# Twice the margin of zero matmuls against the TensorE clock gate, paced by ScalarE, also into the emptied P.V bank

## Chip, cores, metric

The kernel runs on one core of a Trainium2 chip. The metric is the device time of one execution in microseconds (us), as a median over timed executions. The granted clock of TensorE is 1.000 at full speed. PE is TensorE, ACT is ScalarE, DVE is VectorE, POOL is GpSimd. All kernels in this document gave correct outputs.

## The reference, cut to what matters

There are two identical layers on a sequence of 2048 rows of 512: multi-query attention with 32 heads of 16, then a gated MLP that mixes over the sequence.

```python
x = x + _A_ref(_layernorm(x), wq, wk, wv, wo)       # 32 heads, one K and one V of width 16
x = x + _B_ref(_layernorm(x), w_in, w_sp, b_sp, w_out)
x = x + _A_ref(_layernorm(x), wq, wk, wv, wo)
x = x + _B_ref(_layernorm(x), w_in, w_sp, b_sp, w_out)
# _A_ref: scores = q k^T / 4, p = softmax(scores), o = p v, then o @ wo
# _B_ref: z = gelu(x @ w_in); z1, z2 = halves; g = w_sp @ layernorm(z2) + b_sp; (z1 * g) @ w_out
```

The exponentials (32 x 2048 x 2048 in each layer) are the bulk of the work.

## The kernel before

The program is not written by hand in order. A list scheduler in the kernel file holds a model of five engines, with an assumed duration for every operation. It simulates them and emits each engine's instructions in the order in which the model started them. PE's list gets its scores (`fill`), the products P.V (`pv`), the background matmuls (projections and the mix over the sequence), and a filler: multiplications of a zero matrix, whose only purpose is to keep PE busy enough for full clock.

```python
TICK = 3.4133            # us, the window in which the model counts PE's columns
TICK_COLS = 3060.0       # columns in a window that the model takes to be enough for full clock
...
def below(self, t, lim):
    # earliest time from t on at which the columns of the last TICK us are under lim
    ...
    return t
...
WARM = 800.0             # margin over TICK_COLS
...
class WarmStream:        # the zero matmuls
    def peek(self, f):
        ...
        t = sc.below(f, TICK_COLS + WARM)
        if u >= len(k.units) or k.units[u].first:       # between two groups: P.V is being emptied
            free = [b for b in sc.banks if not b.busy and not b.closed and b.free_at <= t]
            if not free:
                return None                             # no bank to write to: no zeros
            self.bank = free[0]
        if not sc.fast(t):
            return (t, -1.0)                            # priority: ahead of everything
        return (t, 0.6)                                 # ahead of most background matmuls

    def commit(self, t):
        ...             # inside a group a zero matmul adds zero to P.V's own bank
        pace = []
        if t > k.sc.free["pe"] + 0.3:
            pace = [d for en in ("act", "dve") for d in k.sc.order[en][-8:] if t - 1.5 < d.vis <= t]
            pace = sorted(pace, key=lambda d: -d.vis)[:1]
        o = k.sc.op("pe", fn, 512 / 2400.0, [k.c_zero] + pace + ..., 9.0, sem="warm")
```

`pace` makes a zero matmul wait for the operation that the model finished last before it, so that zeros don't run off early. ACT exponentiates three or two score blocks of 128x512 at a time out of two rings in PSUM. DVE takes about one block in eight and computes it by a polynomial, for which it reads the scores (line L1558) and runs five more instructions for each pair of blocks.

The softmax here doesn't subtract the row's maximum and nothing guards it: scores larger than these inputs give would overflow.

Of the kernel before, what the change touches and what calls it, by code (L numbers as in the profile page):

```python
# [28 lines left out]
TICK_COLS = 3060.0  # L29
# [28 lines left out]
class Sched:  # L58
# [96 lines left out]
        return o  # L155

    def _arm(self, o):
        o.ready = max([d.end if d.eng == "pe" and o.eng == "pe" else d.vis for d in o.deps], default=0.0)
        self.ready[o.eng].append(o)
        self.cache.pop(o.eng, None)  # L160
        for e, _f, _d in o.alts:
            self.ready[e].append(o)
            self.cache.pop(e, None)
# [4 lines left out]
    def _pick(self, eng):  # L168
# [3 lines left out]
        for o in self.ready[eng]:  # L172
# [8 lines left out]
            if r < INF:  # L181
                late = o.unit is not None and o.unit < self.unit_now() + NEAR
                cands.append((r, 0.1 if late else o.prio, o.seq, o, 0.0))
# [187 lines left out]
NDB = 2  # L371

LOOK = 8
NEAR = 4
URGENT = 1.0
BACKLOG = 3.0
WARM = 800.0
ENDX = 6
PR_LAST = 0.3
PR_SMALL = 0.6  # L380
# [6 lines left out]
def d_psum(n):  # L387
    return n * 1.042e-3 + 0.066
# [6 lines left out]
def d_act(n):  # L395
    return n * 0.8333e-3 + 0.051
# [27 lines left out]
class Kern:  # L424
    def __init__(self, nc, A_x, A_wq, A_wk, A_wv, A_wo, B_x, B_w_in, B_w_sp, B_b_sp, B_w_out, out):
# [15 lines left out]
        sc = self.sc = Sched([5, 7])  # L441
# [67 lines left out]
        self.evac_n = 0  # L509
        self.hT_read = [[], []]  # L510
        self.pv_evac = None

        self.load(A_x, A_wq, A_wk, A_wv, A_wo, B_b_sp)
        self.fill_s = FillStream(self)
# [29 lines left out]
        return self.ps16[:, 1024 * b:1024 * (b + 1)]  # L544

    def transpose(self, out, src, deps, sem, pr):
        return self.sc.op("sp", lambda e: e.dma_start_transpose(out, src), 1.2, deps, pr, sem=sem, dma=131072, lat=0.9)

    def dma(self, fn, deps, sem, nbytes, prio=5.0, eng="sp", issue=0.5):
        return self.sc.op(eng, fn, issue, deps, prio, sem=sem, dma=nbytes)  # L550
# [77 lines left out]
    def ln(self, tiles, deps_t, dst, dst_deps, pr, urgent=False, on_pe=False):  # L628
        sc = self.sc
        n = len(tiles)  # L630
        t0 = tiles[0]
        ag = []
        for t in tiles:
            s_ = sc.op("dve", lambda e, t=t: e.bn_stats(self.st1[:, t, :], self.X[:, t, :]), 0.6, deps_t(t),  # L634
                       pr + 0.5)
            ag.append(sc.op("dve", lambda e, t=t: e.bn_aggr(self.mv1[:, t, :], self.st1[:, t:t + 1, :]), 0.13, [s_],
                            pr + 0.4))
        a = sc.op("dve" if urgent else "pool", lambda e: e.tensor_scalar(
            self.ve1[:, t0:t0 + n], self.mv1[:, t0:t0 + n, 1], LN_EPS, None, op0=ALU.add), 0.08 if urgent else 0.25, ag, pr)
        r = sc.op("pool", lambda e: e.tensor_tensor(self.rs1[:, t0:t0 + n], self.ve1[:, t0:t0 + n],  # L640
                                                    self.mhalf[:, 0:1].to_broadcast([P, n]), ALU.pow),
                  0.3 + 0.17 * n, [a, self.c_mh], pr)
        xo = []
        slots = []
        for t in tiles:
            sl = self.xn_n % 4
            self.xn_n += 1
            slots.append(sl)
            xo.append(sc.op("dve", lambda e, t=t, sl=sl: e.tensor_scalar(
                self.xn[:, sl, :], self.X[:, t, :], self.mv1[:, t, 0:1], self.rs1[:, t:t + 1], op0=ALU.subtract,  # L650
                op1=ALU.mult), 0.22, [r, self.last_xn[sl]], pr + 0.3))

        if not urgent and not on_pe:
            evs = []
            for i, (t, sl) in enumerate(zip(tiles, slots)):
                o = self.transpose(dst[:, i, :, :], self.xn[:, sl, :], [xo[i]] + dst_deps, f"xt{sl}", pr)
                self.last_xn[sl] = o
                evs.append(o)
            return evs

        def pe(e, b):
            ins = None
            for i, sl in enumerate(slots):
                for kd in range(KD):
                    k = i * KD + kd
                    ins = e.transpose(self.b16(b)[:, k * 128:(k + 1) * 128], self.xn[:, sl, kd * 128:(kd + 1) * 128],
                                      self.ident[:])
            return ins

        def cp(b):  # L670
            return dst, self.b16(b)[:, 0:n * 512].rearrange("p (t kd c) -> p t kd c", t=n, kd=KD)
        pt, (ev,) = sc.job([(pe, n * 4 * 0.06)], [dict(
            fn=lambda e, b: e.tensor_copy(*cp(b)), dur=d_psum(n * 256), prio=pr, deps=dst_deps,
            alts=[("act", lambda e, b: e.activation(*cp(b), ACTF.Copy), d_act(n * 512) + 0.1)])], xo + [self.c_id], pr)
        for sl in slots:
            self.last_xn[sl] = pt
        return [ev]
# [240 lines left out]
    def mixer_chunk(self, g):  # L918
        sc = self.sc
        n = g.n  # L920
        nt = n // 128
        T = [g.t0 // 128 + i for i in range(nt)]
        last = (g.ci == len(self.chunks) - 1)
        pr = PR_LAST if last else (PR_SMALL if g.ci >= 3 else 3.0)
# [9 lines left out]
        for i, t in enumerate(T):  # L934
            for h in range(2):
# [8 lines left out]
                def cp(b, t=t, h=h):  # L944
# [6 lines left out]
                                         deps=list(self.z2_read.get(t, ())),  # L951
# [16 lines left out]
        for f0 in range(0, NF, per):  # L968
# [10 lines left out]
            def cp(b, f0=f0, m=len(fs)):  # L979
# [5 lines left out]
                                for i in range(0, len(mm), w)],  # L985
                               [con] if last else [dict(fn=lambda e, b, cp=cp: e.tensor_copy(*cp(b)), dur=d_psum(n * len(fs)), prio=pr - 1,  # L986
                                     deps=z1_war,
# [12 lines left out]
        nt = len(T)  # L1000
# [16 lines left out]
        for ci, (zt, zn, v) in zip(batch, zs):  # L1017
            sp = self.dma(lambda e, zt=zt, zn=zn, v=v: e.dma_start(self.z1_dv[:, :, zt * 128:zt * 128 + zn], v), z1,
                          f"z1s{g.layer}{zt}", zn * P * NF * 2)
# [9 lines left out]
        for t in T:  # L1029
# [3 lines left out]
        a = sc.op("dve" if last else "pool", lambda e: e.tensor_scalar(  # L1033
            self.ve2[:, T[0]:T[0] + nt], self.mv2[:, T[0]:T[0] + nt, 1], LN_EPS, None, op0=ALU.add), 0.08 if last else 0.25,
            ag, pr)
        r = sc.op("pool", lambda e: e.tensor_tensor(self.rs2[:, T[0]:T[0] + nt], self.ve2[:, T[0]:T[0] + nt],
                                                    self.mhalf[:, 0:1].to_broadcast([P, nt]), ALU.pow),
                  0.3 + 0.17 * nt, [a], pr)
        for t in T:
            self.z2_op[t] = sc.op("dve", lambda e, t=t: e.tensor_scalar(  # L1040
                self.z2n[:, t, :], self.z2n[:, t, :], self.mv2[:, t, 0:1], self.rs2[:, t:t + 1], op0=ALU.subtract,
# [201 lines left out]
class FillStream:  # L1243
# [26 lines left out]
    def peek(self, f):  # L1270
        k = self.k
        r = self.n % 2
        if self.pending[r]:
            return None
        self.blocks = self.nxt(k.ring[r][1])
        if not self.blocks:
            return None
        deps = [self.exp_of[r]]
        for b in self.blocks:
            g = b.unit.grp  # L1280
            if g.q.op is None or g.q.op.start is None:
                return None
            deps.append(g.q.op)
            o = k.k_op.get((g.layer, b.unit.kt))
            if o is None or o.start is None:
                return None
            deps.append(o)
        if not k.sc.reclaim(r):
            return None
        self.deps = [d for d in deps + k.sc.lent_rel(r) if d is not None]  # L1290
        return (max([d.vis for d in self.deps], default=0.0), 0.0)
# [173 lines left out]
class DexStream:  # L1465
# [28 lines left out]
    def take(self, t, js):  # L1494
# [27 lines left out]
        layer = k.units[fu].grp.layer  # L1522
        u = max(self.u, fu + LOOK)
        while u < len(k.units):
# [117 lines left out]
class WarmStream:  # L1642
# [10 lines left out]
    def peek(self, f):  # L1653
        k = self.k
        sc = k.sc
        u = k.pv_s.u
        self.bank = None
        if sc.nleft == 0 or k.c_zero.start is None:
            return None
        f = max(f, k.c_zero.vis)  # L1660
        t = sc.below(f, TICK_COLS + WARM)
        if u >= len(k.units) or k.units[u].first:
            free = [b for b in sc.banks if not b.busy and not b.closed and b.free_at <= t]
            if not free:
                return None
            self.bank = free[0]
        if not sc.fast(t):
            return (t, -1.0)
        return (t, 0.6)

    def commit(self, t):
        k = self.k
        b = self.bank

        def fn(e):
            return e.matmul(k.b32(k.pvb if b is None else b.idx), k.zero[:], k.zero[:, None, :].to_broadcast([P, 4, P]),  # L1676
                            start=b is not None, stop=b is not None)
        pace = []
        if t > k.sc.free["pe"] + 0.3:
            pace = [d for en in ("act", "dve") for d in k.sc.order[en][-8:] if t - 1.5 < d.vis <= t]  # L1680
            pace = sorted(pace, key=lambda d: -d.vis)[:1]
        o = k.sc.op("pe", fn, 512 / 2400.0, [k.c_zero] + pace + (b.rel if b is not None else []), 9.0, sem="warm")
        k.sc.commit(o, t)
        if b is not None:
            b.rel = [o]
            b.free_at = o.end
        self.n += 1
# [59 lines left out]
```

## Time and profile before

| | before |
|---|---|
| timed executions when the prediction was made | 1846.22 us median of 3 (1843.32 to 1848.53) |
| the profiled execution | 1860.4 us (span 1858.4 us, granted clock 0.983) |
| zero matmuls | 786 |
| ACT busy in the profiled execution | 1746.0 us of 1858.4 |

These lines are from the page of the profiled execution of before: busy time by engine, the granted clock in 40 slices (tenths), and two of the costliest groups (busy us, mean ns | idle time ahead of them, and what ended it).

```profile
span 1858.4 us, 30069 instructions
...
PE 1599.4 (86%) x11874; PEld 473.0 (25%) x11874; DVE 1700.6 (92%) x2912; ACT 1746.0 (94%) x1570; POOL 52.4 (3%) x90
...
PEclk9899999999999999998999999999999999999999
...
L1374 ACT ACTIVATE Pa<-ps_all 128x1536 bf16<-128x1536 f32 (+1 forms) x1433 | 1631.8, 1372 | 32.6 <-PE ps_all L1694 30.8
...
L1676 PE MATMUL ps_all<-zero 128*128 128x512 bf16 x786 | 257.8, 399 | 34.9 <-DVE mv L1032 7.2
...
```

ACT is 94% busy. Its exponentials (L1374) take 1631.8 us and wait 30.8 us for scores. The clock row is 8 in two slices only; its tenths hide most of what is below 1.

The next lines are busy times in seven stretches of the same execution: first:last us and length, then PE, weight loads, DVE, ACT and POOL, each busy (xinstructions), then PEclk, the DMA share and GB/s. The stretches are the start, the first 16 groups of attention, groups 17 to 24 (here the first gelus and layer norms of the mixer come in between), the rest of the first layer, the first 8 groups of the second layer, the rest of its attention, and the last stage.

```profile
...
0.00:14.40 14.40, 11.39 (x70) 5.12 (x70) 13.02 (x37) 6.88 (x14) 7.29 (x20) 1.00 0.92 286
14.40:426.90 412.50, 335.93 (x2654) 91.28 (x2653) 391.56 (x632) 406.47 (x364) 5.75 (x11) 0.98 0.19 49
426.90:656.00 229.10, 204.78 (x1457) 57.32 (x1457) 205.33 (x338) 220.12 (x186) 6.62 (x6) 0.96 0.08 23
656.00:922.80 266.80, 240.80 (x1741) 80.44 (x1740) 230.92 (x433) 239.71 (x226) 10.17 (x18) 0.98 0.17 46
922.80:1154.20 231.40, 188.10 (x1424) 52.51 (x1422) 210.65 (x361) 214.62 (x201) 5.94 (x12) 0.99 0.06 14
1154.20:1805.90 651.70, 571.40 (x4271) 164.09 (x4272) 605.58 (x1011) 641.41 (x552) 15.49 (x22) 0.99 0.10 28
1805.90:1858.40 52.50, 47.02 (x262) 22.27 (x260) 43.59 (x109) 16.84 (x34) 1.10 (x2) 1.00 0.32 97
...
```

The same view in windows of 3.41 us shows one cold spell:

```profile
...
51.20:54.61 3.41, 2.85 (x29) 0.76 (x27) 3.31 (x5) 3.13 (x4) 0.00 (x0) 1.00 1.15 346
54.61:58.02 3.41, 2.08 (x15) 0.35 (x12) 3.34 (x6) 2.70 (x3) 0.00 (x0) 0.70 1.11 280
58.02:61.43 3.41, 3.41 (x15) 0.62 (x11) 3.27 (x5) 2.37 (x3) 0.00 (x0) 0.50 1.15 306
61.43:64.85 3.42, 3.42 (x21) 0.64 (x18) 1.08 (x2) 2.77 (x3) 0.00 (x0) 0.50 1.15 307
64.85:68.26 3.41, 3.21 (x31) 0.67 (x27) 3.11 (x5) 3.15 (x3) 0.00 (x0) 0.80 1.14 304
...
```

The half clock comes on within the second row and goes off within the last one. ACT has 0.7, 1.0, 0.6 and 0.3 us idle in these four windows. Over the whole execution 30 such windows are below full clock; ACT is idle 20.0 us in them. The spells are at half clock and last 3.41, 6.83 or 10.24 us; the cuts above don't lie on their borders, so more cuts are touched.

Two causes of such spells are seen in the timeline (start us, length us, engine, line, operation; in brackets the idle time before it and what ended it). Here zeros wait for a late DVE:

```profile
...
515.11 0.39 PE L1676 MATMUL ps_all<-zero 128*128 128x512 bf16 x1
515.55 3.47 DVE L1040 TENSOR_SCALAR z2n<-z2n,mv,rs 128x896 bf16<-128x896 bf16 x8 [1.56 <-POOL rs L1036]
...
517.38 0.61 PE L1676 MATMUL ps_all<-zero 128*128 128x512 bf16 x1 [1.89 <-DVE z2n L1040]
...
517.92 0.61 PE L1694 MATMUL ps_all<-qs,kT 32*128 32x512 bf16 x3
...
518.58 1.45 ACT L1374 ACTIVATE Pa<-ps_all 128x1536 bf16<-128x1536 f32 x1 [1.59 <-PE ps_all L1694]
...
```

The zero at 517.38 waits 1.9 us for DVE's normalization. The scores (L1694) stand behind it on PE although ACT had read out their bank by 516.1 us, and ACT idles 1.59 us. The Trainium skill ("TensorE: Matmul & The Clock Gate", Part 2, step 1) says that matmuls stay in program order and only weight loads are pulled ahead; this trace agrees.

The other cause is a boundary between two groups, here PE alone. P.V's bank is being emptied, no zero is placed between the scores, and PE idles 0.95 and 0.52 us of two; the clock falls behind it:

```profile
...
148.95 0.39 PE L1694 MATMUL ps_all<-qs,kT 32*128 32x512 bf16 x3
150.29 0.39 PE L1694 MATMUL ps_all<-qs,kT 32*128 32x512 bf16 x4 [0.95 <-ACT Pa L1374]
151.21 0.39 PE L1694 MATMUL ps_all<-qs,kT 32*128 32x512 bf16 x2 [0.52 <-ACT Pa L1374]
...
152.50 1.03 PE L1676 MATMUL ps_all<-zero 128*128 128x512 bf16 x2
...
```

### The profile page before, as it was taken

The numbers are of one execution on the slowest core, as the hardware profiler recorded it, in microseconds if no ns is written. First come the engines' busy times: TensorE is split into PE (matmuls) and PEld (weight loads), VectorE is DVE, ScalarE is ACT, GpSimd is POOL, SyncE is SP. The second block draws the span as 40 slices with busy tenths as digits, with TensorE's granted clock in tenths as the row PEclk, the third lists the DMA queues.
The fourth block names the chain that finished last, engine by engine and source line by source line (L and its number), as shares of the span: only waits on it lengthen the run. The fifth ranks groups of instructions, "written<-read, shape, count | busy, mean of one in ns | idle before, by whom it ended". The sixth has DMA issues, their size and how long they took to land.

```text
span 1858.4 us, 30069 instructions
## 1 busy us (share of the span) xinstructions
PE 1599.4 (86%) x11874; PEld 473.0 (25%) x11874; DVE 1700.6 (92%) x2912; ACT 1746.0 (94%) x1570; POOL 52.4 (3%) x90
## 2 busy tenths in 40 slices
PE   8878788778899999998887787987887899899998
PEld 3221222122222222222431211221122222222324
DVE  8999999999988999985869999999999998998868
ACT  8999999999999999999569999999999999999983
POOL 2000000000000000000010000000000000000000
PEclk9899999999999999998999999999999999999999
DMA  9700010001000021101120000100010000112013
GB/s 271 200 1 1 9 38 1 1 1 23 17 24 24 24 46 44 47 35 55 48 51 1 1 1 5 42 1 1 1 21 15 29 24 26 44 43 72 10 55 110
DMA packets 122963, 68.02 MB, mean 37 GB/s; under 512 B 76996, under 2 KB 119240, under 8 KB 122824
## 3 DMA queue, kind: packets, MB, share of 16 engines
q1 hardware_dynamic: 121240, 65.95, 13.2%
q8 instruction: 94, 1.54, 0.3%
q14 instruction: 45, 0.37, 0.1%
q10 hardware_dynamic: 1584, 0.16, 0.1%
HBM read 30.97 MB, written 17.83 MB: 26 GB/s over the span
## 4 chain that ended last, share of the span: by engine, by line
ACT 39%; DVE 21%; PE 20%; issue 17%; DMA 1%; POOL 1%; ACTq 0%; SPq 0%; POOLq 0%
ACT Pa L1374 38%; PE ps_all L1694 5%; PE ps_all L1116 5%; DVE E L1558 3%; PE ps_all L1450 3%; DVE Pd L1589 3%; DVE E L1587 2%; DVE E L1583 2%; DVE E L1585 1%; PE ps_all L1676 1%; PE ps_all L1208 1%; DVE st L634 1%; PE ps_all L939 1%; DVE gp L1129 1%; DVE st L1030 1%
## 5 line engine op out<-in xcount | busy, mean ns | idle before, releaser
L1374 ACT ACTIVATE Pa<-ps_all 128x1536 bf16<-128x1536 f32 (+1 forms) x1433 | 1631.8, 1372 | 32.6 <-PE ps_all L1694 30.8
L1694 PE MATMUL ps_all<-qs,kT 32*128 32x512 bf16 x4096 | 567.9, 389 | 186.9 <-ACT Pa L1374 173.2
L1558 DVE TENSOR_SCALAR E<-ps_all 128x512 f32<-128x512 f32 x514 | 351.1, 685 | 32.3 <-PE ps_all L1694 28.9
L1694 PEld LDWEIGHTS ps_all<-qs,kT 32*128 32x128 bf16 x4096 | 139.0, 91 | 751.7 <-ACT Pa L1374 691.2
L1450 PE MATMUL ps_all<-Pa,V 128*32 128x512 bf16 x3582 | 326.3, 391 | 0.0
L1589 DVE SCALAR_TENSOR_TENSOR Pd<-E 128x1024 uint16<-128x1024 f32 x259 | 313.5, 1211 | 4.2
L1676 PE MATMUL ps_all<-zero 128*128 128x512 bf16 x786 | 257.8, 399 | 34.9 <-DVE mv L1032 7.2
L1116 PE MATMUL ps_all<-wsT,z2n 128*128 128x512 bf16 x714 | 200.3, 383 | 1.5 <-DVE E L1558 0.5
L1450 PE MATMUL ps_all<-Pd,V 128*32 128x512 bf16 x514 | 182.4, 391 | 0.0
L1585 DVE TENSOR_TENSOR E<-E 128x1024 f16<-128x1024 f16 x259 | 176.6, 682 | 4.7
L1587 DVE TENSOR_TENSOR E<-E 128x1024 f16<-128x1024 f16 x259 | 176.6, 682 | 4.2
L1583 DVE TENSOR_SCALAR E<-E 128x1024 f16<-128x1024 uint16 x259 | 176.6, 682 | 1.6
L1586 DVE TENSOR_SCALAR E<-E 128x1024 f16<-128x1024 f16 x259 | 107.8, 416 | 2.3
L1676 PEld LDWEIGHTS ps_all<-zero 128*128 128x128 bf16 x786 | 59.8, 98 | 171.4 <-issue 83.5
L1129 DVE TENSOR_TENSOR gp<-ps_all,gp 128x512 f16<-128x512 f32 x112 | 75.8, 686 | 28.4 <-PE ps_all L1116 28.3
L1450 PEld LDWEIGHTS ps_all<-Pa,V 128*32 128x32 bf16 x3582 | 64.4, 94 | 121.9 <-issue 118.1
L1116 PEld LDWEIGHTS ps_all<-wsT,z2n 128*128 128x128 bf16 x714 | 54.1, 97 | 95.6 <-issue 55.1
L796 PE MATMUL ps_all<-xnTA,wq_pad 128*128 128x512 bf16 (+2 forms) x384 | 72.5, 315 | 0.9 <-DVE z1s L986 0.3
L939 PE MATMUL ps_all<-w_in_r,xnTB 128*128 128x448 bf16 x256 | 63.2, 359 | 3.7 <-DMA xnTB<-xn 2.8
L975 PE MATMUL ps_all<-xnTB,w_in_r 128*128 128x512 bf16 (+2 forms) x336 | 62.8, 310 | 1.9 <-DVE gp L986 1.0
L1208 PE MATMUL ps_all<-E 128*128 128x512 bf16 x224 | 53.9, 380 | 3.6 <-ACT E L1187 2.8
L1187 ACT ACTIVATE E<-ps_all 128x512 f16<-128x512 f32 (+1 forms) x49 | 23.7, 555 | 28.6 <-PE ps_all L1175 28.6
(89 smaller groups left out, 996.0 us busy)
## 6 DMA issues: line engine op xcount, KB each, us to landing
wsT_scratch<-gp SPq DMA_DIRECT2D x16, 512.0 KB, 3.6
wsT<-wsT_scratch SPq DMA_DIRECT2D x8, 1024.0 KB, 5.4
z1s<-z_scratch SPq DMA_DIRECT2D x16, 448.0 KB, 3.8
wsT<-wsT_scratch SPq DMA_DIRECT2D x8, 512.0 KB, 3.5
z_scratch<-z1s SPq DMA_DIRECT2D x4, 896.0 KB, 5.2
X<-in_A_x_dram SPq DMA_DIRECT2D x8, 256.0 KB, 5.9
out_dram<-X SPq DMA_DIRECT2D x16, 128.0 KB, 2.0
w_in_r<-in_B_w_in_dram SPq DMA_DIRECT2D x1, 1792.0 KB, 10.3
```

The costliest lines, as they stand in the source:

```text
L1116: ins = e.matmul(self.b32(b), self.z2n[:, s, f * 128:(f + 1) * 128], w_[:, s - s0, :] if s - s0 < na or not spare else wsp[:, s - s0 - na, :],
L1129: return e.tensor_tensor(dst, self.b32(b), dst, ALU.add)
L1374: return e.activation(k.Pa[:, base:base + n, :], k.b32(b0, n).rearrange("p (k q) -> p k q", k=n), ACTF.Exp, scale=SCALE)
L1450: ins = e.matmul(k.b32(k.pvb)[32 * j:32 * j + 32, :], k.V[:, u.kt, 32 * j:32 * j + 32], b.slot, tile_position=(0, 32 * j), start=u.first, ...
L1558: c = k.sc.op("dve", lambda e: e.tensor_scalar(k.ey[:, s, 512 * i:512 * (i + 1)], k.b32(j.bank.idx)[:, 0:512], E_LOG2, E_BIAS, op0=ALU.mul ...
L1583: o2 = sc.op("dve", lambda e: e.tensor_scalar(x, lo, E_X * 2.0 ** -16, E_X * E_A, op0=ALU.mult, op1=ALU.add), d_sb(n, 0.521e-3), self.ops ...
L1585: o3 = sc.op("dve", lambda e: e.tensor_tensor(w, x, x, ALU.mult), d_sb(n, 0.521e-3), [o2, self.wfree], pr)
L1586: o4 = sc.op("dve", lambda e: e.tensor_scalar(w, w, E_C, None, op0=ALU.add), d_sb(n, 0.26e-3), [o3], pr)
L1587: o5 = sc.op("dve", lambda e: e.tensor_tensor(w, w, x, ALU.mult), d_sb(n, 0.521e-3), [o4], pr)
L1589: o7 = sc.op("dve", lambda e: e.scalar_tensor_tensor(po.bitcast(U16), y, E_D, w, op0=ALU.add, op1=ALU.add), d_sb(n, 1.042e-3), [o5] + self ...
L1676: return e.matmul(k.b32(k.pvb if b is None else b.idx), k.zero[:], k.zero[:, None, :].to_broadcast([P, 4, P]), start=b is not None, stop=b ...
L1694: return e.matmul(self.b32(bank), self.kT[32 * j:32 * j + 32, kt * 128:(kt + 1) * 128], self.qs[32 * j:32 * j + 32, g.q.slot, :], tile_pos ...
```

## The change

The intent is to have PE at full clock at all times: the margin of zeros over the clock threshold doubles (`WARM` 800 to 1600). Between groups, where no side bank is free, zeros may go into the P.V bank as soon as it has been emptied. Zeros wait for ACT alone, and for DVE only where ACT has finished nothing within 1.5 us. Three assumed durations grow (transposes by DMA, two reciprocal square roots on POOL). `SLACK` and `AHEAD` are zero, so their lines do nothing.

```diff
--- before.py
+++ after.py
@@ -155,7 +155,8 @@
         return o
 
     def _arm(self, o):
-        o.ready = max([d.end if d.eng == "pe" and o.eng == "pe" else d.vis for d in o.deps], default=0.0)
+        sl = SLACK if o.eng == "pe" and o.prio >= 0.9 else 0.0
+        o.ready = max([d.end if d.eng == "pe" and o.eng == "pe" else d.vis + (sl if d.eng in ("dve", "pool", "sp") else 0.0) for d in o.deps], default=0.0)
         self.ready[o.eng].append(o)
         self.cache.pop(o.eng, None)
         for e, _f, _d in o.alts:
@@ -371,10 +372,12 @@
 NDB = 2
 
 LOOK = 8
+SLACK = 0.0
+AHEAD = 0.0
 NEAR = 4
 URGENT = 1.0
 BACKLOG = 3.0
-WARM = 800.0
+WARM = 1600.0
 ENDX = 6
 PR_LAST = 0.3
 PR_SMALL = 0.6
@@ -509,6 +512,7 @@
         self.evac_n = 0
         self.hT_read = [[], []]
         self.pv_evac = None
+        self.pv_bank = Bank(self.pvb)
 
         self.load(A_x, A_wq, A_wk, A_wv, A_wo, B_b_sp)
         self.fill_s = FillStream(self)
@@ -544,7 +548,7 @@
         return self.ps16[:, 1024 * b:1024 * (b + 1)]
 
     def transpose(self, out, src, deps, sem, pr):
-        return self.sc.op("sp", lambda e: e.dma_start_transpose(out, src), 1.2, deps, pr, sem=sem, dma=131072, lat=0.9)
+        return self.sc.op("sp", lambda e: e.dma_start_transpose(out, src), 1.2, deps, pr, sem=sem, dma=131072, lat=1.4)
 
     def dma(self, fn, deps, sem, nbytes, prio=5.0, eng="sp", issue=0.5):
         return self.sc.op(eng, fn, issue, deps, prio, sem=sem, dma=nbytes)
@@ -639,7 +643,7 @@
             self.ve1[:, t0:t0 + n], self.mv1[:, t0:t0 + n, 1], LN_EPS, None, op0=ALU.add), 0.08 if urgent else 0.25, ag, pr)
         r = sc.op("pool", lambda e: e.tensor_tensor(self.rs1[:, t0:t0 + n], self.ve1[:, t0:t0 + n],
                                                     self.mhalf[:, 0:1].to_broadcast([P, n]), ALU.pow),
-                  0.3 + 0.17 * n, [a, self.c_mh], pr)
+                  0.38 + 0.17 * n, [a, self.c_mh], pr)
         xo = []
         slots = []
         for t in tiles:
@@ -1035,7 +1039,7 @@
             ag, pr)
         r = sc.op("pool", lambda e: e.tensor_tensor(self.rs2[:, T[0]:T[0] + nt], self.ve2[:, T[0]:T[0] + nt],
                                                     self.mhalf[:, 0:1].to_broadcast([P, nt]), ALU.pow),
-                  0.3 + 0.17 * nt, [a], pr)
+                  0.3 + 0.23 * nt, [a], pr)
         for t in T:
             self.z2_op[t] = sc.op("dve", lambda e, t=t: e.tensor_scalar(
                 self.z2n[:, t, :], self.z2n[:, t, :], self.mv2[:, t, 0:1], self.rs2[:, t:t + 1], op0=ALU.subtract,
@@ -1658,12 +1662,19 @@
         if sc.nleft == 0 or k.c_zero.start is None:
             return None
         f = max(f, k.c_zero.vis)
-        t = sc.below(f, TICK_COLS + WARM)
+        near = u < len(k.units) and (k.units[u].first or k.units[u].last)
+        t = sc.below(f, TICK_COLS + WARM + (AHEAD if near else 0.0))
         if u >= len(k.units) or k.units[u].first:
             free = [b for b in sc.banks if not b.busy and not b.closed and b.free_at <= t]
-            if not free:
-                return None
-            self.bank = free[0]
+            if free:
+                self.bank = free[0]
+            else:
+                ev = k.pv_s.evac
+                if ev is None or ev.start is None or u >= len(k.units) or k.units[u].grp.layer != k.units[u - 1].grp.layer:
+                    return None
+                t = max(t, ev.vis)
+                self.bank = k.pv_bank
+                self.bank.rel = [ev]
         if not sc.fast(t):
             return (t, -1.0)
         return (t, 0.6)
@@ -1677,7 +1688,8 @@
                             start=b is not None, stop=b is not None)
         pace = []
         if t > k.sc.free["pe"] + 0.3:
-            pace = [d for en in ("act", "dve") for d in k.sc.order[en][-8:] if t - 1.5 < d.vis <= t]
+            pace = [d for d in k.sc.order["act"][-8:] if t - 1.5 < d.vis <= t] or \
+                [d for d in k.sc.order["dve"][-8:] if t - 1.5 < d.vis <= t]
             pace = sorted(pace, key=lambda d: -d.vis)[:1]
         o = k.sc.op("pe", fn, 512 / 2400.0, [k.c_zero] + pace + (b.rel if b is not None else []), 9.0, sem="warm")
         k.sc.commit(o, t)
```

As the order comes from the model, any of these lines re-makes the order of the whole program: PE's list goes from 786 to 1182 zeros, and DVE's and ACT's orders change too.

## The prediction

> **What bounds the kernel now.** By the table of busy time per stretch, ScalarE (ACT) is busy 779.7 of 796 us in the first attention stage (50 to 846 us) and 783.5 of 793 in the second (975 to 1768); VectorE (DVE), which takes a share of the exponentials, 746.5 and 754.6. ACT is the bound there. In the closing stages (846 to 975, 1768 to 1858) ACT is idle 41 and 37 us. The chain of waits says ACT 39%, DVE 21%, PE 20%, issue 17%.
>
> **What is to be won.** The granted clock is 0.983. Cut into slices of 3.41 us, 30 slices have a clock of 0.5 to 0.8, in 12 episodes. The Trainium skill, "TensorE: Matmul & The Clock Gate", section "The HAM clock gate", says PE runs at half clock after an idle window of about 3.4 us; the trace agrees roughly: episodes follow gaps of 1 to 2 us and last 2 to 4 slices. In these slices ACT is idle 20.0 us and DVE 32.8; at the rate of the other attention slices (0.024 and 0.166 us) it would be 0.7 and 5. So at most 19 us of ACT and 28 of DVE are lost to the slow clock and the gaps that cause it. A block's exponential costs DVE 685 ns + half of 3085 = 2.2 us, ACT about 0.55, so 28 us of DVE are worth about 7 of ACT; shared by both, all is worth about 20 us (1.1%).
>
> **What the change does** (instruction order of both):
> 1. Zero matmuls go from 786 to 1182, in every stage. One takes about 0.21 us of PE back to back, so 396 add about 85 us, in gaps. PE is in order: a score matmul just behind one starts up to 0.2 us later. Scores fill two rings in turn, which hides most: 2 to 4 us lost.
> 2. At group boundaries (timeline at 151, 351, 1078, 1310 us) PE has no bank for zeros while P.V's is emptied, and goes cold. Zeros now go there: these four episodes (9 slices) should vanish, 4 us with DVE's part.
> 3. Zeros that wait for DVE fall from 157 to 62. At 515 us one waits 1.9 us for DVE's z2n line, and ACT idles 1.6 and 1.2 us: 4 to 6 us won.
> 4. The assumed latency of transposes goes from 0.9 to 1.4 us, so consumers stand later in PE's order. At 1160 us PE waits 1.06 us for such a DMA and ACT 2.19: 2 to 4 us won.
> 5. SLACK and AHEAD are 0 and do nothing. ACT's exponentials stay 1433, DVE's about 258 batches: no work moves.
>
> Episodes that will partly stay: 54 to 68 us (loads), 447 (DMA), 853 and 1775 (table loads and layer norm before closing). The closing stages hardly change.
>
> **Predicted:** 1830 us, range 1811 to 1848; faster by over 2%: 0.08, within 2%: 0.89, slower by over 2%: 0.03. That is 16 to 18 us won of 20, 2 to 4 lost, a little from point 4.
>
> **What would show it.** Clock 0.990 to 0.997; cold slices 30 down to 5 to 15; PE busy up 100 to 150 us (modelled ends, 389 ns each); ACT idle 112 us down to about 95; ACT's exponentials unchanged at 1632 us; ACT's wait for scores (30.8 us) down to about 20.
>
> **What would make it wrong.** Zeros in front of scores where real time runs late against the scheduler's: ACT's wait for scores then rises though the clock is 1.0. The schedule is re-made as a whole, so closing stages may shift 5 to 10 us either way. Zeros tied to ACT alone may let PE run dry where ACT is late.

## The result

| | before | after |
|---|---|---|
| timed, first measurement | 1845.78 us (1843.32 to 1848.53, 4 runs) | 1840.71 us (1840.08 to 1841.71, 4 runs) |
| ratio after : before | | 0.9973 (0.9955 to 0.9990) |
| profiled execution: span, clock | 1858.4 us, 0.983 | 1838.4 us, 0.998 |
| ACT idle in it | 112.4 us | 94.5 us |
| zero matmuls | 786 | 1182 |

A ratio is the mean time of one kernel's fast runs over that of the other kernel's fast runs of the same rounds, so it is not quite the ratio of the medians. The record marks an execution as slow when its time stands well above the others of its kernel; all executions here are marked fast.

The change won 5.1 us in the medians. I had predicted 16, with a range that ended at 1811 to 1848; the measured time lies in the range, but the gain is a third of the one forecast. Yet from profile to profile the gain is 20.0 us, a little more than predicted. So two questions stand: where the 15 us between these two gains are, and what the change really is worth.

The page of after, the same lines:

```profile
span 1838.4 us, 30853 instructions
...
PE 1655.8 (90%) x12185; PEld 509.7 (28%) x12270; DVE 1700.0 (92%) x2906; ACT 1743.9 (95%) x1571; POOL 50.2 (3%) x90
...
PEclk9999999999999999999999999999999999999999
...
L1378 ACT ACTIVATE Pa<-ps_all 128x1536 bf16<-128x1536 f32 (+1 forms) x1433 | 1629.5, 1370 | 9.7 <-PE ps_all L1706 8.6
...
L1687 PE MATMUL ps_all<-zero 128*128 128x512 bf16 x1182 | 363.4, 388 | 12.1 <-DVE st L1034 3.9
...
```

The clock row is 9 throughout, the exponentials cost the same (1629.5 us), and their wait for scores fell from 30.8 to 8.6 us. The same seven stretches of after (borders at the same events, so at other times):

```profile
...
0.00:18.00 18.00, 15.00 (x77) 6.76 (x78) 16.62 (x44) 6.37 (x13) 8.07 (x21) 0.91 0.87 279
18.00:425.60 407.60, 358.10 (x2788) 101.45 (x2787) 392.01 (x629) 406.78 (x364) 4.58 (x10) 1.00 0.20 47
425.60:642.00 216.40, 198.60 (x1457) 60.08 (x1471) 206.54 (x344) 214.95 (x182) 4.42 (x6) 1.00 0.08 24
642.00:908.30 266.30, 246.16 (x1754) 83.47 (x1777) 227.97 (x424) 241.24 (x225) 12.23 (x18) 0.99 0.16 46
908.30:1140.30 232.00, 201.28 (x1500) 59.81 (x1503) 213.95 (x368) 214.96 (x204) 5.94 (x12) 1.00 0.06 14
1140.30:1785.40 645.10, 588.41 (x4353) 175.18 (x4390) 599.25 (x996) 641.89 (x553) 13.81 (x22) 1.00 0.10 28
1785.40:1838.40 53.00, 48.22 (x265) 22.93 (x267) 43.67 (x109) 17.71 (x36) 1.10 (x2) 1.00 0.32 96
...
```

Row by row against before the lengths differ by +3.6, -4.9, -12.7, -0.5, +0.6, -6.6 and +0.5 us, together -20.0. Two thirds are won in the third stretch, where the clock was 0.96 and is 1.00. This part is no bad luck of the profiled execution. A second trace of before was kept later, of an execution at a clock of 0.990 (run b_again, span 1849.1 us), and its third stretch is as long and as cold:

```profile
...
422.90:652.30 229.40, 201.79 (x1439) 57.29 (x1457) 205.26 (x337) 220.08 (x186) 6.63 (x6) 0.96 0.08 23
...
```

Of the 20.0 us, 9.3 thus lie between two executions of before, in other stretches (4.0 in the second, 2.6 in the fourth, 2.4 in the sixth), and 10.7 between that second one and after. Something is lost at the start: the first exponential comes at 18.0 us and not at 14.4 (at 16.4 in after's second trace, which has no half clock there).

A place where zeros wait for DVE in after (matmuls of PE and one instruction of ACT):

```profile
...
509.31 1.47 PE L1687 MATMUL ps_all<-zero 128*128 128x512 bf16 x6 [0.71 <-ACT z2n L1014]
...
511.62 2.59 PE L1687 MATMUL ps_all<-zero 128*128 128x512 bf16 x10 [0.84 <-DVE st L1034]
...
515.00 1.68 PE L1687 MATMUL ps_all<-zero 128*128 128x512 bf16 x7 [0.78 <-DVE st L1034]
...
516.73 4.62 ACT L1378 ACTIVATE Pa<-ps_all 128x1024 bf16<-128x1024 f32 x4
...
517.81 0.39 PE L1706 MATMUL ps_all<-qs,kT 32*128 32x512 bf16 x2 [1.12 <-ACT Pa L1378]
...
```

ACT runs gelus of 3.17 us each there and seldom finishes anything, so zeros still wait for DVE (L1034), for 0.8 us each time. But they come 6, 10 and 7 in a row, and the clock holds.

The group boundary, in after:

```profile
...
150.02 0.39 PE L1687 MATMUL ps_all<-zero 128*128 128x512 bf16 x1
150.66 0.40 PE L1706 MATMUL ps_all<-qs,kT 32*128 32x512 bf16 x4 [0.26 <-ACT Pa L1378]
150.99 0.39 PE L1687 MATMUL ps_all<-zero 128*128 128x512 bf16 x1
151.36 0.40 PE L1454 MATMUL ps_all<-Pa,V 128*32 128x512 bf16 x3
...
152.34 0.82 PE L1687 MATMUL ps_all<-zero 128*128 128x512 bf16 x3
```

Zeros stand between the scores now, and PE's longest idle time in it is 0.26 us. The view doesn't tell which bank they write to. In the built program, of 1182 zeros only 18 use the emptied P.V bank, at 12 of the 64 boundaries; 128 use a side bank, the others add to P.V.

### The profile page after: what moved, and what is told of

Read it like the earlier page. It is cut to its first block, busy times and chain, and to the rows that moved or that the text cites. A ratio compares the mean times of both kernels' runs of the same rounds, so it can differ in the third digit from the quotient of the medians.

```text
span 1838.4 us, 30853 instructions
## 1 busy us (share of the span) xinstructions
PE 1655.8 (90%) x12185; PEld 509.7 (28%) x12270; DVE 1700.0 (92%) x2906; ACT 1743.9 (95%) x1571; POOL 50.2 (3%) x90
## 4 chain that ended last, share of the span: by engine, by line
ACT 41%; PE 24%; DVE 17%; issue 17%; POOL 0%; DMA 0%; ACTq 0%; another core or an unknown queue 0%; SPq 0%; POOLq 0%
ACT Pa L1378 39%; PE ps_all L1706 6%; PE ps_all L1120 6%; PE ps_all L1454 4%; DVE E L1562 3%; DVE Pd L1593 2%; PE ps_all L1212 2%; PE ps_all L1687 2%; DVE E L1589 1%; DVE E L1587 1%; DVE E L1591 1%; DVE gp L1133 1%; PE ps_all L943 1%; DVE st L638 1%; DVE E L1590 1%
## 5 line engine op out<-in xcount | busy, mean ns | idle before, releaser
L1378 ACT ACTIVATE Pa<-ps_all 128x1536 bf16<-128x1536 f32 (+1 forms) x1433 | 1629.5, 1370 | 9.7 <-PE ps_all L1706 8.6
L1706 PE MATMUL ps_all<-qs,kT 32*128 32x512 bf16 x4096 | 561.9, 385 | 140.8 <-ACT Pa L1378 123.4
L1687 PE MATMUL ps_all<-zero 128*128 128x512 bf16 x1182 | 363.4, 388 | 12.1 <-DVE st L1034 3.9
L1120 PE MATMUL ps_all<-wsT,z2n 128*128 128x512 bf16 x656 | 187.3, 382 | 5.8 <-issue 3.0
L1687 PEld LDWEIGHTS ps_all<-zero 128*128 128x128 bf16 x1182 | 90.7, 98 | 197.1 <-issue 136.8
L1120 PEld LDWEIGHTS ps_all<-wsT,z2n 128*128 128x128 bf16 x714 | 55.6, 97 | 94.7 <-issue 55.5
```

Source lines behind the costliest of these rows:

```text
L1120: ins = e.matmul(self.b32(b), self.z2n[:, s, f * 128:(f + 1) * 128], w_[:, s - s0, :] if s - s0 < na or not spare else wsp[:, s - s0 - na, :],
L1378: return e.activation(k.Pa[:, base:base + n, :], k.b32(b0, n).rearrange("p (k q) -> p k q", k=n), ACTF.Exp, scale=SCALE)
L1687: return e.matmul(k.b32(k.pvb if b is None else b.idx), k.zero[:], k.zero[:, None, :].to_broadcast([P, 4, P]), start=b is not None, stop=b ...
L1706: return e.matmul(self.b32(bank), self.kT[32 * j:32 * j + 32, kt * 128:(kt + 1) * 128], self.qs[32 * j:32 * j + 32, g.q.slot, :], tile_pos ...
```

## The experiments

Two theories stood at first. "Sample": the profiled execution of before was an unlucky one, and a typical one has less to be won. "Cost": the 20 us are there in every execution, and the additional zeros and the new order lose most of them again. The labels beginning with b_ are made from before, those with a_ from after. The "clock line" of the last column is explained under b_again; a kernel's distance from it is taken at the means of its time and clock, not at the median. The column "clock" is the mean over executions. All outputs are right.

| label | zeros | clock | median us | ratio to before (95%) | off the clock line, us |
|---|---|---|---|---|---|
| b_again | 786 | 0.988 | 1851.6 | 1.0007 (0.9984 to 1.003) | (part of the line) |
| b_warm | 1158 | 0.995 | 1846.6 | 0.9979 (0.9961 to 0.9998) | +1.4 |
| b_bank | 770 | 0.994 | 1836.9 | 0.9923 (0.9905 to 0.9941) | -9.9 |
| b_pace | 786 | 0.993 | 1842.3 | 0.9958 (0.9940 to 0.9977) | -4.7 |
| b_est | 779 | 0.989 | 1853.1 | 1.0003 (0.9980 to 1.0026) | +1.3 |
| b_bankpace | 770 | 0.996 | 1836.1 | 0.9901 (0.9880 to 0.9922) | -9.5 |
| bp_warm12 | 970 | 0.996 | 1840.7 | 0.9935 (0.9909 to 0.9962) | -4.1 |
| a_again | 1182 | 0.998 | 1840.4 | 0.9952 (0.9933 to 0.9971) | -2.1 |
| a_startest | 1188 | 0.999 | 1840.6 | 0.9958 (0.9937 to 0.9979) | -0.1 |
| a_oldpace | 1182 | 0.999 | 1839.5 | 0.9947 (0.9925 to 0.9968) | -2.6 |
| a_oldest | 1182 | 0.999 | 1840.5 | 0.9929 (0.9913 to 0.9946) | -1.0 |
| a_warm8 | 802 | 0.989 | 1857.2 | 1.0015 (0.9996 to 1.0033) | +4.8 |
| a_warm14 | 1044 | 0.997 | 1841.6 | 0.9943 (0.9922 to 0.9964) | -2.2 |
| a_warm18 | 1326 | 1.000 | 1850.0 | 0.9989 (0.9968 to 1.001) | +9.4 |
| a_warm24 | 1875 | 0.999 | 1900.2 | 1.0251 (1.0230 to 1.0273) | +59 |
| a_warm32 | 3382 | 0.997 | 2181.8 | 1.1797 (1.1770 to 1.1825) | (far off) |

### b_again: the kernel before once more

No edit.

> The kernel before once more, for its spread and the granted clock of each execution. Theory 'sample': the profiled execution of before (span 1858 us, clock 0.983) was an unlucky one; the timed ones (1843 to 1848) have a clock of 0.988 to 0.993, and over executions the time falls by some 1.2 to 2 us per 0.001 of clock; so from the typical execution only 8 to 12 us were there to be won, not 20. Theory 'cost': the timed executions have a clock near 0.983 as well (profiling alone makes the 12 us), and the change wins about 18 us and loses 12 to its zeros and its new order. Both expect a ratio to before of 1.000.

Measured: 1851.6 us (1847.13 to 1860.61) for this copy and 1851.02 us (1846.15 to 1856.33, 11 runs) for before beside it. With before's runs beside the later experiments there are 46 executions of the same instructions, on four chips, and each has a clock:

| granted clock | executions | mean us | lowest to highest us |
|---|---|---|---|
| 0.981 to 0.985 | 6 | 1857.2 | 1855.4 to 1860.6 |
| 0.986 to 0.989 | 20 | 1853.0 | 1850.7 to 1856.3 |
| 0.990 to 0.992 | 13 | 1850.4 | 1847.1 to 1854.1 |
| 0.993 to 0.997 | 7 | 1845.9 | 1843.3 to 1848.0 |

A straight line through the 46 has a slope of 1.03 us per 0.001 of clock (correlation -0.92, 1.4 us of scatter around it). It gives 1857.8 us at 0.983, 1851.7 at the mean clock of 0.989, and 1842.5 at after's 0.998. This is the clock line of the table.

The two traces of before show that the clock is the cause here, and not some late instruction that makes PE cold and ACT late alike. From 45 us to 56.2 us every instruction of PE, ACT and DVE starts at the same time in both, to 0.01 us. Then the clock is half in the first trace, from 56.0 to 66.2 us, and stays full in b_again's, as these rows for two of the windows shown above say:

```profile
...
54.61:58.02 3.41, 2.08 (x19) 0.51 (x19) 3.34 (x6) 3.14 (x3) 0.00 (x0) 1.00 1.11 297
58.02:61.43 3.41, 2.82 (x24) 0.81 (x21) 3.27 (x5) 3.24 (x4) 0.00 (x0) 1.00 1.12 290
...
```

ACT comes out of that spell 2.4 us later. The half clock starts on a grid of 3.41 us in both traces, and the grid lies 0.26 us earlier in b_again's, counted from the first instruction. In all the first trace has 19 windows at half clock and b_again's 11, and the spans differ by 9.3 us, 1.2 us for a window; by the line of the 46 it would be 0.95.

The same program thus takes anything from 1843 to 1861 us, by how many cold windows it meets. Profiling itself costs nothing that shows: b_again's profiled execution took 1851.06 us, the median of its six 1851.6. The profiled 1860.4 us at 0.983 is the second longest of all, and 14.6 us over the median of the timed runs that lay beside it. So "sample" holds: most of those 14.6 us were in the saving that I read from the trace, and not in the median that I took it from. "Cost" wanted the timed executions to have a clock near 0.983 too; six of 46 do. My expected slope of 1.2 to 2 was somewhat high.

### a_again: the kernel after once more

No edit.

> The kernel after once more. Over 18 executions of before the time falls 1.17 us per 0.001 of clock (correlation -0.91), from 1858.8 at 0.983 to 1841 at 0.998. Theory 'sample': after is 1839 to 1842 with a clock of 0.997 to 0.998 and a spread under 3 us on any chip, and the ratio hangs on the clock that before happens to get: 0.994 to 0.995 where before has about 0.989, 0.997 where it has 0.993. Theory 'cost': the ratio is 0.997 again and before and after differ at equal clock.

Measured: 1840.44 us (1840.03 to 1841.50), clock 0.997 or 0.998 in each of six executions, against 1850.99 us (1843.27 to 1855.69) for before: ratio 0.9952. After's time stays where it was in the first measurement (1840.71), while before's moved by 5 us. After lies 2.1 us under the clock line of before. After's clock is thus worth some 9 us over before's mean clock, and something else, perhaps the new order of the program, about 2 more: 10.6 us by these medians. The first measurement's 5.1 us had four executions of before at 1843 to 1848, which on the line would be clocks of 0.992 to 0.997; that is an estimate, for their clocks are not on record. Which executions of before stood beside after was chance.

### b_warm: the margin alone

```diff
-WARM = 800.0
+WARM = 1600.0
```

> Before with only WARM 800 to 1600 (1158 zeros). Theory 'sample': clock 0.993 to 0.997, 3 to 7 us faster than before, nearly no contention. Theory 'cost': the clock rises by 0.010 and the time falls by 5 us or less, or rises, and ACT's wait for scores grows.

Measured: 1846.64 us, ratio 0.9979, clock 0.992 to 0.997. It is 4.4 us faster and 1.4 us over the clock line, with 372 more zeros. So the zeros bring about what the clock brings, and no cost of the size that "cost" had wanted is seen. A smaller cost isn't excluded: the order was re-made too, and the runs below scatter by several us at equal clock.

### b_bank: the P.V bank alone

```diff
-            if not free:
-                return None
-            self.bank = free[0]
+            if free:
+                self.bank = free[0]
+            else:
+                ev = k.pv_s.evac
+                ...                     # as in the change
+                t = max(t, ev.vis)
+                self.bank = k.pv_bank
+                self.bank.rel = [ev]
```

> Before with only zeros into the emptied P.V bank (770 zeros). Both theories: the cold episodes at group boundaries go; 2 to 5 us faster, clock up by 0.002 to 0.004.

Measured: 1836.91 us (1835.83 to 1837.87), ratio 0.9923, at a clock of 0.993 to 0.994. It is 14 us faster than before, three times what I expected, and faster than the whole change. But only 8 of its 770 zeros use the P.V bank, at 6 of the 64 boundaries; the clock accounts for some 4 us, and 9.9 us are beyond the clock line. What these few zeros did is to shift the model a little, and with it the order of everything after: DVE's list has 2909 operations in place of 2912, PE's 4407 in place of 4421. I name this "order scatter" below. That the order makes the 9.9 us is argued from what is left over; no run tests it by itself. Both theories had missed it.

### b_pace: the pacing alone

```diff
-            pace = [d for en in ("act", "dve") for d in k.sc.order[en][-8:] if t - 1.5 < d.vis <= t]
+            pace = [d for d in k.sc.order["act"][-8:] if t - 1.5 < d.vis <= t] or \
+                [d for d in k.sc.order["dve"][-8:] if t - 1.5 < d.vis <= t]
```

> Before with only the pacing by ACT: the order of every engine is the same, only the waits of zeros differ. If late DVE waits at the head of PE's queue matter as I predicted (4 to 6 us), this alone is 3 to 6 us faster and the 1.6 us idle of ACT near 517 us goes; if they seldom matter, within 1.5 us of before. Zeros may run earlier than planned and so leave later windows cold: then it is slower and the clock is lower.

Measured: 1842.27 us, ratio 0.9958. This is the cleanest of the single parts, for the orders of ACT and DVE are the same as before's, line by line, and PE's is too; 42 zeros wait for DVE in place of 157. The clock rises to 0.989 to 0.994, and 4.7 us are beyond the clock line. From the waits of ACT, this is the line of b_again (for us in total, times, longest) and then that of b_pace:

```profile
...
ACT Pa L1374 <- PE ps_all L1694: 22.3, 43, 2.3
...
```

```profile
...
ACT Pa L1374 <- PE ps_all L1695: 17.8, 33, 1.9
...
```

The total falls by 4.5 us; these are single executions with 11 and 8 windows at half clock, so a part of it can be the clock's. The place that I had named is healed: ten exponentials run from 503.99 to 515.39 us without a pause, past DVE's normalization that had held a zero and the scores behind it. The third stretch, whose order is that of before, has full clock now and is 7.0 us shorter than in b_again:

```profile
...
424.60:647.00 222.40, 194.69 (x1439) 56.46 (x1457) 204.87 (x337) 219.19 (x186) 6.64 (x6) 1.00 0.08 23
...
```

By these traces, zeros that waited for a late DVE did both, hold scores back and let PE go cold. My 4 to 6 us for this point were, on before, somewhat low. And 4.7 us off the clock line without any new order show that not everything off the line is order.

### a_oldpace: the change without its pacing

```diff
-            pace = [d for d in k.sc.order["act"][-8:] if t - 1.5 < d.vis <= t] or \
-                [d for d in k.sc.order["dve"][-8:] if t - 1.5 < d.vis <= t]
+            pace = [d for en in ("act", "dve") for d in k.sc.order[en][-8:] if t - 1.5 < d.vis <= t]
```

> After with the old pacing (ACT or DVE, whichever the plan has last); the order of all engines is that of after. On before, the new pacing alone gave about 8 us, of which about half at equal clock. If that holds beside the larger margin: 3 to 6 us slower than after, clock 0.993 to 0.997, ACT's wait for scores back to 20 us. If the margin alone already covers the late waits: within 1.5 us of after.

Measured: 1839.49 us (1837.07 to 1841.35), ratio 0.9947, clock 0.997 to 1.000. It is not slower than after; my expectation of 3 to 6 us fell. The order is after's, and 158 zeros wait for DVE again (64 in after; both counted from the semaphores in the traces). So beside the larger margin the pacing is worth nothing: the gains of the parts do not add up. The third stretch, for one, has full clock in b_pace, in b_warm and in a_oldpace alike. The lines of the waits of after and of a_oldpace show how little there is left to win:

```profile
...
ACT Pa L1378 <- PE ps_all L1706: 8.6, 29, 0.9
...
```

```profile
...
ACT Pa L1378 <- PE ps_all L1705: 7.7, 27, 0.9
...
```

### b_est and a_oldest: the estimates alone, and all but them

```diff
-... sem=sem, dma=131072, lat=0.9)            # b_est; a_oldest is the reverse
+... sem=sem, dma=131072, lat=1.4)
-                  0.3 + 0.17 * n, [a, self.c_mh], pr)
+                  0.38 + 0.17 * n, [a, self.c_mh], pr)
-                  0.3 + 0.17 * nt, [a], pr)
+                  0.3 + 0.23 * nt, [a], pr)
```

> Before with only the three estimates. a_oldest (after without them) had 1840.5, the same as after, so they should be worth nothing by themselves: time on the line of before (1851 at 0.9895, 1.0 us per 0.001 of clock) within 4 us, with the late first exponential (16.4 us or later) and PE's waits for the onT transposes (11 us before) gone.

> After with all three estimates (transposes, both POOL) put back: what is left are the margin, the bank and the pacing. If the longer transpose estimate is worth 2 to 4 us, as I predicted, this is 2 to 4 us slower than after; if the estimates only re-made the order, it lies anywhere within 4 us of after, 1836 to 1844, with a clock of 0.997 to 1.0.

Measured: b_est 1853.13 us, ratio 1.0003, clock 0.988 to 0.992; a_oldest 1840.50 us (1839.93 to 1840.85) at 0.998 to 1.000, the time of after. In b_est the first exponential comes at 16.4 us, as expected. PE's waits for the transposed `onT` (6.1 us of weight loads and 4.8 us of matmuls in before's profile) are gone in b_est, so the estimates did what they are for. But the whole did not gain. Beside b_again's trace the third stretch of b_est is 8.4 us shorter and the sixth 1.9, while the last is 5.8 us longer, the second 3.2, the fifth 2.3 and the start 2.0. In the last stage stand 60 matmuls of the mix over the sequence (L1116), 21 in b_again: the re-made order moved them there, without more zeros. My 2 to 4 us for this point were not seen.

### a_startest: one estimate put back, for the start

```diff
-                  0.38 + 0.17 * n, [a, self.c_mh], pr)
+                  0.3 + 0.17 * n, [a, self.c_mh], pr)
```

> After with only the first POOL estimate put back (0.38 to 0.3), which brings DVE's order in the first 14 us back to that of before. If that estimate made the late start (first exponential at 18.0 us in place of 14.4, and a half-clock window behind it), the first exponential is at 14.4 us again, that window is gone, and the whole is 3 to 6 us faster than after: 1835 to 1838. If the start is made up later, or the re-made schedule moves more than this, it lies within 2 us of after or beyond it either way.

Measured: 1840.58 us (1839.76 to 1845.06), ratio 0.9958. The first exponential is at 14.4 us again, so this estimate did make the late start. But the whole is no faster: the 24th group ends at 642.3 us, in after's second execution at 640.5. What the start wins is lost by then. In this execution a cold window with 2.2 us of ACT idle stands at 519 us. A loss at one place of the program is not a loss at its end when everything behind it is re-ordered. My expectation fell.

### a_warm8, a_warm14, a_warm18, a_warm24, a_warm32: after with other margins

```diff
-WARM = 1600.0
+WARM = 3200.0        # a_warm32; 800.0, 1400.0, 1800.0, 2400.0 in the others
```

> After with WARM 3200: 3382 zeros, 2200 more than after, about 460 us more of PE. The clock can gain no more than 0.002, so this measures what zeros cost. Theory 'cost' (396 zeros lose about 10 us): 40 to 60 us slower than after. Theory 'sample' (they cost nearly nothing where ACT is the bound): under 12 us slower, ACT's wait for scores up by less than that.

> After with the old margin of 800 (802 zeros, 380 fewer). If the doubled margin is what brings the clock from 0.994 to 0.998 and the zeros cost nothing: clock 0.992 to 0.995 and 3 to 6 us slower than after (1843 to 1846, by 1.0 us per 0.001 of clock). If its zeros cost what the clock brings: within 2 us of after. If they cost more: 1835 to 1838.

> After with a margin of 2400 (1875 zeros, 693 more than after, about 146 us more of PE). a_warm32 lost 341 us with 2200 more, 0.155 us each. If a zero always costs that: 107 us slower than after, and then the 396 of the change cost 61 us, which can't be. If they cost only where PE has no room left: 3 to 30 us slower, most of it in the closing stages.

> After with a margin of 1400 (1044 zeros, 138 fewer). It re-makes the order without taking away what the zeros are for. If the order alone scatters the time by several us, this lies 2 to 6 us from after (1840.5) on either side at a clock of 0.995 to 0.999; if after's 4 us behind b_bank is what its extra zeros cost, it lies between: 1837 to 1840.

> After with a margin of 1800 (1326 zeros, 144 more). If zeros cost from here on as between 1600 and 2400 (60 us for 693): about 12 us slower than after, with more than 21 of L1120's matmuls left for the last stage. If the cost sets in later: within 3 us of after.

| margin | zeros | clock | median us | matmuls of the mix over the sequence (L1120) in the last stage |
|---|---|---|---|---|
| 800 | 802 | 0.989 | 1857.2 | 21 |
| 1400 | 1044 | 0.997 | 1841.6 | 21 |
| 1600 | 1182 | 0.998 | 1840.4 | 21 |
| 1800 | 1326 | 1.000 | 1850.0 | 57 |
| 2400 | 1875 | 0.999 | 1900.2 | 98 |
| 3200 | 3382 | 0.997 | 2181.8 | 345 |

Below 1600 the clock falls. Above it, zeros become dear: by the medians 144 more lose 9.5 us, 693 more lose 60 us (0.09 us each), 2200 more lose 341 us (0.16 us each). The clock cannot be the cause, for it is 1.000 at 1800. These lines are groups of PE instructions in the last stage, first of after, then of a_warm24 (busy us, mean ns | idle before):

```profile
...
L1120 PE MATMUL ps_all<-wsT,z2n 128*128 128x512 bf16 x21 | 5.0, 379 | 0.0
L1687 PE MATMUL ps_all<-zero 128*128 128x512 bf16 x18 | 4.4, 380 | 0.6 <-DVE ve L642 0.5
...
```

```profile
...
L1120 PE MATMUL ps_all<-wsT,z2n 128*128 128x512 bf16 x99 | 24.3, 379 | 0.2
...
L1687 PE MATMUL ps_all<-zero 128*128 128x512 bf16 x14 | 3.7, 381 | 1.1 <-DVE X L1217 0.6 <-DVE E L1194 0.6
...
```

The last stage has fewer zeros in a_warm24 than in after, but 99 matmuls of the mix where after has 21 (one of the 99 starts a moment before the stage as the table counts it). The stage takes 72.8 us in place of 53.0. More than half of the loss lies at the end of the first layer: there 61 matmuls of the mix come after the second layer has begun (none in after), and the fifth stretch takes 266.7 us in place of 232.0. A zero has a better priority than these background matmuls. When zeros take PE's room during attention, the background work stays behind and comes at the end of the layer, where attention no longer hides it. So a zero costs nothing that is seen here as long as it fills a gap that nobody wanted, and 0.09 to 0.16 us on the mean where zeros displace work. The margin of 1600 lies just on the safe side. At the size of the change "cost" finds no support: its own 396 zeros left the number at 21, and after lies under the clock line, not over it.

Against the expectations: a_warm18 came out as its first case said (9.5 us lost, about 12 expected). For a_warm24 (60 us) and a_warm32 (341 us) none of my cases was large enough, and a_warm14 lies 1.1 us from after, nearer than the 2 to 6 us that I had given to the order.

a_warm8 missed on the other side: 11 to 14 us slower than I had expected, and 4.8 us over the clock line. In its profiled execution the stretch after the layer boundary takes 240.9 us where after's second execution has 232.0, with three windows below full clock at 911 to 921 us. Six matmuls of the mix come behind the layer boundary there, and none in after; which of the two makes the loss is not shown.

### b_bankpace and bp_warm12: can more be had?

```diff
-WARM = 800.0         # b_bankpace: bank and pacing alone; bp_warm12: this line too
+WARM = 1200.0
```

> Before with zeros into the emptied P.V bank and pacing by ACT, margin still 800: the order of every engine is that of b_bank (1836.9 us, clock 0.994). Pacing gave 8.7 us on before and nothing on after. If it helps wherever windows are still cold: clock 0.995 to 0.998 and 2 to 4 us faster than b_bank (1833 to 1835). If what it did on before was only to cure the waits that the bank change cures too: within 1.5 us of b_bank.

> Before with the bank and the pacing by ACT at a margin of 1200 (970 zeros), no new estimates. b_bankpace has 1836.1 at 0.996. If the missing 0.002 to 0.003 of clock can be had without other loss: 1832 to 1835 at 0.998 to 1.0, the best of all. If the order scatters the time: 1833 to 1843.

Measured: b_bankpace 1836.11 us (1833.66 to 1836.95), ratio 0.9901, clock 0.994 to 0.997: with b_bank, from which it can't be told apart (0.8 us, within the 1.5 us of my second case), the best of all, and better than after, whose ratio beside another set of before's runs is 0.9952. It has b_bank's order. bp_warm12, meant to be better still, has 1840.69 us at about the same clock, as the case "the order scatters the time" had it. So their difference of 4.6 us is not clock. Six kernels with 970 to 1188 zeros and a clock of 0.996 or more (after, a_startest, a_oldpace, a_oldest, a_warm14, bp_warm12) lie 0 to 4 us under the clock line, b_bank and b_bankpace nearly 10 under it, b_warm 1.4 and a_warm8 4.8 over it. Why the order of b_bank is the good one is not settled. In the profiled executions b_bank wins against after 4.2 us in the first 8 groups of the second layer, 3.6 at the start and 1.4 before the layer boundary, and loses 3.1 us in the third stretch and 2.6 in the sixth.

## Why the prediction was right or wrong

The prediction had the mechanism and mis-sized the first term of its sum.

- **What failed** is the step "What is to be won", with its "the whole" of "about 20 us", and "16 to 18 us won of 20" in the last sum. The 30 cold windows and the 20.0 us of idle ACT belong to one execution of 1860.4 us at a clock of 0.983. I subtracted their repair from the 1846 us median of other executions. A typical execution of before has 0.989, and the clock line gives 9.2 us up to after's clock (1851.7 less 1842.5). The two measurements of the gain, 5.1 us in the first and 10.6 us in the second, lie around that; how far the first fell below it was chance, by the executions of before that it met. From profile to profile, where the subtraction is a right one, it is 20.0 us, of which 9.3 lie between two executions of before and 10.7 between the more typical of them and after.
- **The warning stood on record.** The profiled execution was 14 us longer than the median of the timed ones, nearly as much as the gain that I forecast. And the Trainium skill ("TensorE: Matmul & The Clock Gate", Part 1, The HAM clock gate) says of the number of cold matmuls at the start of a kernel that "it's run-variable", because the window runs free. I cited that section for the half clock and did not use this sentence. What it says of the start is seen here over the whole run: clocks of 0.981 to 0.997 from the same instructions in 46 executions, and grids of half clock that lie 0.26 us apart in the two traces of before.
- **Clock and spells:** right, and better than predicted. Clock 0.998 (I had 0.990 to 0.997); the windows below full clock went from 30 to 4 (I had 5 to 15); ACT's wait for scores from 30.8 to 8.6 us (I had 20); ACT idle 112.4 to 94.5 us (I had 95); exponentials 1629.5 us, unchanged.
- **Point 1, 2 to 4 us lost to the zeros:** not seen, but with orders that scatter by more than this not excluded. b_warm is 1.4 us over the clock line, after 2.1 us under it, and the wait for scores fell. PE's busy time rose by 56.4 us and not by 100 to 150; the group of zeros alone rose by 105.6 us, from 257.8 to 363.4, while matmuls at half clock, which count longer, went away. After's trace also lacks the records of some 85 matmuls (12185 beside 12270 weight loads), so its sum is a little low.
- **Point 2, the bank, 4 us:** the boundaries I named are no longer cold, but only 18 zeros use the P.V bank. Alone it gave 14 us, of which 9.9 are off the clock line and probably the re-made order's, so the 4 us can neither be confirmed nor refuted.
- **Point 3, the pacing, 4 to 6 us:** the place and the mechanism were right: 7.8 us on before by the ratio (0.0042 of 1851), and in the traces the third stretch alone is 7.0 us shorter. Beside the doubled margin, which heals the same place, none.
- **Point 4, the estimates, 2 to 4 us:** nothing in the whole; the waits on DMA went, and what the third stretch won was lost in others.
- **"Closing stages may shift 5 to 10 us either way"** was the only place that I gave to the re-made order. Stretches all over the program moved, and kernels with up to 1188 zeros lie -10 to +5 us off the clock line. Most of this is probably order, but not all: b_pace, at -4.7 us, has the order of before.

What stays open: what is good about the order of b_bank, and which clocks the four executions of before had in the first measurement.

## What to carry to other kernels

Subtract a saving from the execution in which you read it. Where a profiled execution and the timed median of the same program differ by as much as the gain that you forecast, first find out what the time depends on from run to run (here the granted clock: 1.03 us per 0.001), and predict from the typical execution. Filler work is free only as long as it takes gaps: check that background work has not moved to the end of a layer. And when a scheduler re-makes the order, a test of one line of the change tests a new program too, so compare several neighbours before you credit the line.

## What the Trainium skill lacked or had wrong

- "TensorE: Matmul & The Clock Gate" says that the ramp penalty is "<1% of a typical kernel span"; this is about the warm-up at the start. Of cooling during a run the page has cases, but no figure for how much the time of one program then varies. Here it varied between executions by 17.3 us, 0.94% (1843.3 to 1860.6 us), in step with the clock. The page gives no way to size this from one trace; 46 executions gave it.
- The same page's table of goals asks for "No PE-idle gaps >~3µs between matmul bursts". Here gaps of 0.95 and 0.52 us within two microseconds, and one of 1.9 us, already stood in front of spells at half clock. In the 3.41 us ahead of each of before's 11 spells PE was idle for 1.1 to 2.7 us, never for all of it. So where the prediction says that the trace "agrees roughly", this holds for the half clock and for the length of the spells (whole multiples of 3.41 us), and not for the idle window. The page has no figure for how much activity within a window is enough.
- No page has the cost of filler matmuls: in this program no cost was seen with 1182 of them, and 0.09 us each on the mean for the next 693.
